# Clustered attention with an ELU network: the order of three kinds of VectorE work, and two blocks' row sums moved to VectorE

## The chip, the cores and the metric

The kernel runs on one core of a Trainium2 chip. The core has a matrix engine (TensorE, PE in the profile; its weight loads are listed as PEld), VectorE (DVE), ScalarE (ACT), GpSimd (POOL) and SyncE (SP, which only issues transfers here). Each engine works through its own list of instructions in order and waits on semaphores for the others. The metric is the device time of one execution in microseconds, lower is better.

## The reference

Inputs: q, k, v of shape (4 batches, 8 heads, 768 tokens, 64), 16 centroids a head, and two weight matrices 512 x 2048 and 2048 x 512. All are float64; the kernel turns them into float32.

```python
q_assign = np.argmax(np.einsum('bhsd,hcd->bhsc', q_n, c_n), axis=-1)   # q_n, k_n, c_n: normalised
k_assign = np.argmax(np.einsum('bhsd,hcd->bhsc', k_n, c_n), axis=-1)
mask = q_assign[:, :, :, None] == k_assign[:, :, None, :]
scores = np.where(mask, scale * q @ k^T, -1e9)
attn = exp(scores - max) / (sum + 1e-9)
x = (attn @ v), heads side by side                     # 3072 tokens x 512
h = x @ w_in
g = np.where(h > 0, h, np.exp(np.minimum(h, 0)) - 1)   # ELU
out = g @ w_out
```

A token of q attends only to the tokens of k that fall into the same cluster.

## The kernel before, in words

The work is cut into 48 blocks: 4 batches, 3 thirds of the queries (256 each), 4 pairs of heads. The loop at L795 runs over n, and each turn writes out by hand what every engine does next; no scheduler moves anything. In turn n:

- `values(n - 1)` multiplies the exponentials of the block before with v into `o_bank` (L581), and needs the sum of each row of exponentials. Either PE forms it with a matrix of ones (`row_sums`, L570: 12 small matmuls a block), or `sums(n)` has formed it on VectorE in three additions (L558, L559, L560, into the tile `psum`), and PE needs 2 matmuls. Then ScalarE (L599 to L602), VectorE (L603, L604) and POOL (L607) divide by the sum.
- `scores(n)` multiplies q and k in three units of 1024 columns (L499; in batch 0 also the mask, L511), each into one of three pairs of PSUM banks, and ScalarE takes the exponential (L522). In the later batches VectorE zeroes the other clusters afterwards (L457).
- `turn` transposes the q and k of the next batch on VectorE (L342).
- The network of the third that is LAG = 7 blocks back comes in groups of steps, four turns to a third. `hidden` (L617) multiplies x with a quarter of w_in into a pair of PSUM banks (L622), ScalarE takes the exponential (L632), POOL clips it (L633), and `elu` on VectorE joins the two (L639) and forms a difference (L641 or L643). The ELU is not issued at once: it is put on the list `lag`, and issued by the next `finish()`, which the next `hidden`, a step of its own, or the next turn calls. The ELU frees the PSUM banks of its slice. Two slices come in the turns with n - 7 divisible by 4, the other two and a `finish` in the turn after.
- `outer` (L660) then forms the product with w_out by seven products of halves instead of eight (L652), four in the third turn and three in the fourth. They use sums and differences of quarters of w_out (`sum_weights`, L322): t1, t2 and t4 in `w_sum`, and f_ overwritten by h_ - f_ in `w_out`. The third product needs the new f_, the fourth t4. The results pass through `o_bank` and `f_bank`, which ScalarE and VectorE empty (L686, L692, L697, L702); L687 and L693 update the ELU's halves.

The weights arrive as float64 words and are turned into float32 on VectorE and ScalarE in 34 steps (`weight_steps`, L265); `weigh(i)` issues i of them, three a turn in `scores` (L554) and some more in the turns 0, 7 and 8. In turn 8 `sum_weights` follows, in two halves, after all steps of the network.

Where `sums` stands in a turn: it is `late`, from turn 10 on, issued ahead of the network's steps or, in some turns, among them. At the end of a batch (turns 11, 23, 35; `extra[1]`, L857) VectorE is asked, after the second `hidden` of the turn, for the clusters of the next batch: `tell(b + 1, 0)` for q, the similarities of k (`clusters`: PE L377, VectorE L384), and `tell(b + 1, 1)` for k. A `tell` is six instructions on VectorE (twice L396, L400, L410) that leave `hot`. The next turn's `values` and `scores` follow, then `key_numbers` (L425), which reads k's `hot`, and `query_numbers` (L438).

Three pairs of banks go round. In the turn after a batch's end (12, 24, 36) the third unit of scores writes the pair that the second `hidden` of the turn before has used; in turn 9 the third unit writes the pair of the fourth `hidden` of turn 8 (L801, L803).

Of the kernel before, what the change touches and what calls it, by code (L numbers as in the profile page):

```python
# [15 lines left out]
Alu = mybir.AluOpType  # L16
# [45 lines left out]
def main_path(ctx, tc, c, q, k, v, centroids, moe_w_in, moe_w_out, out):  # L62
    nc = tc.nc
# [34 lines left out]
    def banks(i=None):  # L98
        nonlocal turn_of
        if i is None:  # L100
            i = turn_of
            turn_of = (turn_of + 1) % 3
        return pair_tiles[i % 3]
# [66 lines left out]
    for e in range(2):  # L170
# [5 lines left out]
            op=Alu.add,  # L176
# [27 lines left out]
    for e in range(2):  # L204
# [11 lines left out]
        op=Alu.mult,  # L216
# [90 lines left out]
    def weigh(n):  # L307
        for _ in range(n):
            next(rest, None)
# [7 lines left out]
    def w_parts():  # L317
        e_, f_ = w_out[:, : FC // 2, :QS], w_out[:, : FC // 2, QS:]
        g_, h_ = w_out[:, FC // 2 :, :QS], w_out[:, FC // 2 :, QS:]
        return e_, f_, g_, h_  # L320

    def sum_weights(half):  # L322

        of = slice(half * FC // 4, (half + 1) * FC // 4)
        e_, f_, g_, h_ = (x[:, of] for x in w_parts())
        t1, t2, t4 = (w_sum[:, n, of] for n in range(3))
        nc.vector.tensor_tensor(t1, f_, e_, op=Alu.subtract)
        nc.gpsimd.tensor_tensor(f_, h_, f_, op=Alu.subtract)
        nc.vector.tensor_tensor(t2, h_, t1, op=Alu.subtract)
        nc.vector.tensor_tensor(t4, g_, t2, op=Alu.subtract)  # L330

# [83 lines left out]
    def side(pr, e):  # L415
        return int(pr // 2 != e)
# [66 lines left out]
    LAG = 7  # L483
# [7 lines left out]
    def scores(n):  # L491
        b, third, pr = blocks[n]
        i = b * NPR + pr
        cols = ts(third, QS)

        def plain(s, kt):
            for e in range(2):
                rows = slice(64 * e, 64 * e + 64)
                nc.tensor.matmul(  # L499
                    s[:, e, ts(kt % 2, QS)],  # L500
                    lhsT=T[i, 1][rows, ts(kt, P)],
                    rhs=T[i, 0][rows, cols],
                    start=n > 0 or kt % 2 == 0,
                    stop=b > 0,
                    skip_group_check=n == 0,
                )

        def mask(s, kt):
            for e in range(2):
                rows = slice(64 * e, 64 * e + 64)  # L510
                nc.tensor.matmul(  # L511
                    s[:, e, ts(kt % 2, QS)],
                    lhsT=hot[b, 1][rows, side(pr, e), ts(kt, P)],
                    rhs=qm[n][rows],
                    start=False,
                    stop=True,
                    skip_group_check=n == 0,
                )

        def exponentials(s, u):  # L520
            p = pu[n, u] = probs.tile([P, 2, 2 * QS], F32, name="p", tag="p")
            nc.scalar.activation(p, s, Act.Exp, scale=SCALE)  # L522

        if n == 0:

            turn_first = similar(0, 1, 0, QS, o_bank)
            turn_rest = similar(0, 1, QS, 2 * QS, f_bank)
            units = [banks() for _ in range(2)]
            for u in range(2):
                for m in range(2):  # L530
                    plain(units[u], 2 * u + m)
            turn_first()
            for u in range(NT // 2):
                assign(0, 1, u * QS, QS)
                if u == 0:
                    turn_rest()
                if u == 1:
                    units.append(banks())
                    for m in range(2):
                        plain(units[2], 4 + m)  # L540
                for m in range(2):
                    mask(units[u], 2 * u + m)
                exponentials(units[u], u)
                weigh(1)
            return
        for u in range(NT // 2):
            s = banks(place["u"][u])
            for m in range(2):
                plain(s, 2 * u + m)
                if b == 0:  # L550
                    mask(s, 2 * u + m)
            exponentials(s, u)
            if n < LAG + 3:
                weigh(1)  # L554

    def sums(n):
        to = osum[n] = work.tile([P, 2, 2 * QS], F32, name="psum", tag="psum", bufs=1)
        nc.vector.tensor_tensor(to, pu[n, 0], pu[n, 1], op=Alu.add)  # L558
        nc.vector.tensor_tensor(to, to, pu[n, 2], op=Alu.add)  # L559
        nc.vector.tensor_tensor(to[:, :, :QS], to[:, :, :QS], to[:, :, QS:], op=Alu.add)  # L560
# [51 lines left out]
    def finish():  # L612
        for step in lag:
            step()
        lag.clear()
# [126 lines left out]
    def clusters(b, j, i):  # L742
        ps = banks(i)
        for turn_half in [similar(b, j, half * HS, HS, ps[:, half]) for half in range(2)]:
            turn_half()

    def tell(b, j):
        for half in range(2):
            assign(b, j, half * HS, HS)
# [45 lines left out]
    for n in range(len(blocks) + LAG):  # L795
        b, at = n // NB, n % NB
        ahead = b + 1 < B

        kind = (n - LAG) % 4 if n >= LAG else None
        if kind == 1:  # L800
            place.update(d=at_tile, u=[at_tile + 1, at_tile, at_tile + 2], h=[at_tile + 1, at_tile])  # L801
        elif kind == 2:
            place.update(d=at_tile + 2, u=[at_tile + 1, at_tile + 2, at_tile])  # L803
        else:
            place.update(d=at_tile, u=[at_tile + 1, at_tile + 2, at_tile])
            place.update(h=[at_tile + 1, at_tile + 2])
        if kind not in (0, 1):
            at_tile += 1
        if n > LAG:
            finish()  # L810
        if n <= len(blocks) and n > 0:
            values(n - 1)
        finish()
        if ahead:
            for pr in {5: [0], 6: [1], 9: [2], 10: [3]}.get(at, []):
                load("q", (b + 1) * NPR + pr)
                load("k", (b + 1) * NPR + pr)
        if n + 1 < len(blocks):
            load_v(n + 1)
        early = 0 < n < LAG + 3  # L820
        more = n + 1 < len(blocks) and at + 1 < NB
        if more and early:
            masks(n + 1)
        if n < len(blocks):
            scores(n)
        if more and not early:
            masks(n + 1)
        if n == 0:
            weigh(3)
        if n < len(blocks):  # L830
            if ahead and at in turns:
                for j in range(2):
                    turn((b + 1) * NPR + turns[at], j)
        main = groups[n - LAG] if n >= LAG else []
        extra = {}
        if n < len(blocks):
            late = [lambda n=n: sums(n)] if n >= LAG + 3 else []
            if b > 0:
                third = at // NPR
                q_in = lambda b, third, places: (lambda: query_numbers(b, third, places))  # L840
                if at == 0:
                    key_numbers(b)
                    query_numbers(b, third, [(0, o_bank)])
                    extra[0] = [q_in(b, third, [(1, f_bank), (2, o_bank)])]
                    extra[1] = [q_in(b, third, [(3, f_bank)])]
                elif at % NPR == 0:
                    query_numbers(b, third, [(0, f_bank), (1, o_bank)])
                    extra[0] = [q_in(b, third, [(2, f_bank), (3, o_bank)])]
                keep_same(n)
            if b > 0 and at % NPR == 2:  # L850
                extra[1] = late
            elif not ahead or at + 1 < NB:
                late and late[0]()
        if ahead and at + 1 == NB:

            extra[0] = [lambda b=b, i=place["u"][2]: clusters(b + 1, 0, i)] + late
            extra[1] = [  # L857
                lambda b=b: tell(b + 1, 0),
                lambda b=b, i=place["h"][0]: clusters(b + 1, 1, i),
                lambda b=b: tell(b + 1, 1),  # L860
            ]
        for m, step in enumerate(main):
            step()
            for other in extra.get(m, []):
                other()
            if n < LAG + 2 and m < 2:
                weigh(2 if n == LAG else 1)
        if n == LAG + 1:
            weigh(100)
            for half in range(2):  # L870
                sum_weights(half)
        if n == len(blocks) + 1:
            findings()
        if n == len(blocks) + 2:
            verdict()
# [254 lines left out]
```

## Time and profile before

| | |
|---|---|
| median of 8 runs | 1010.68 us |
| lowest, highest | 1009.28, 1013.11 us |
| the eight | 1011.15, 1010.20, 1010.98, 1012.61, 1009.91, 1010.38, 1009.28, 1013.11 |
| the profiled execution | 1013.1 us, its span 1010.9 us |
| mean granted clock of TensorE | 0.992 |
| PE busy | 990.1 us (98%) |
| VectorE busy | 657.3 us (65%) |
| ScalarE busy | 322.8 us (32%) |
| POOL busy | 135.5 us (13%) |
| L570 with p, 240 records | 37.2 us |
| L570 with psum, 152 records | 22.9 us |

A float32 matmul leaves two records, so that 12 row-sum matmuls are 24 records. All times in the trace are microseconds from the start of the span. In a timeline a row gives start, duration, engine, line, operation, output <- inputs, shapes and how often; a bracket gives how long the engine stood idle before it, and what ended that. Turns 8, 9 and 10 of the loop lie at about 108 to 132, 132 to 155 and 155 to 174 us. The three ends of a batch lie at about 188 to 208, 430 to 448 and 668 to 686 us.

### The profile page before, as it was taken

What the parts mean: (1) busy time and instruction counts of PE and PEld (TensorE: products, weight loads), DVE (VectorE), ACT (ScalarE), POOL (GpSimd) and SP (SyncE); (2) the same over time, 40 slices, a digit from 0 to 9 for tenths busy, and PEclk for the clock granted to TensorE, in tenths of its full rate; (3) what the DMA queues carried; (4) which work ended last, traced back from release to release, by engine and by line L of the source; (5) the groups of instructions that cost most, each with busy time, mean ns of one, the idle gap of its engine ahead of it and who ended that gap; (6) DMA issues with size and microseconds to landing.
All of it is one profiled execution on the core that took longest, in us unless ns stands there. A gap on an engine that the chain in (4) does not pass through costs nothing.

```text
span 1010.9 us, 14691 instructions
## 1 busy us (share of the span) xinstructions
PE 990.1 (98%) x5989; PEld 774.2 (77%) x5989; DVE 657.3 (65%) x1182; ACT 322.8 (32%) x576; POOL 135.5 (13%) x145
## 2 busy tenths in 40 slices
PE   6999999999999999999999999999999999999997
PEld 4566777767877877868788788777887887888886
DVE  7999973556756766787567467677666665673131
ACT  6777422223233232223232232124224223321010
POOL 0010130110210210111111111111021021021010
PEclk9899999989999999999999999999999999999999
DMA  9857122001123122100122113010011010100000
GB/s 290 315 162 191 56 53 63 18 16 32 37 47 64 37 48 48 52 17 17 53 43 52 39 39 70 30 27 29 16 38 31 17 37 17 32 21 1 22 1 24
DMA packets 103962, 55.58 MB, mean 55 GB/s; under 512 B 83408, under 2 KB 96720, under 8 KB 103888
## 3 DMA queue, kind: packets, MB, share of 16 engines
q1 hardware_dynamic: 103888, 54.57, 19.8%
q8 instruction: 49, 0.80, 0.3%
q14 instruction: 25, 0.20, 0.1%
HBM read 48.27 MB, written 6.29 MB: 54 GB/s over the span
## 4 chain that ended last, share of the span: by engine, by line
PE 81%; DVE 15%; issue 1%; ACT 1%; DMA 0%; POOL 0%; SPq 0%; DVEq 0%; POOLq 0%; ACTq 0%
PE banks L622 29%; PE f_bank L652 16%; PE o_bank L652 12%; PE banks L499 10%; PE o_bank L581 10%; PE banks L570 2%; DVE ex L272 2%; DVE gT L639 1%; DVE w_in L275 1%; DVE w_out L275 1%; DVE w_in L278 1%; DVE ex L294 1%; DVE w_out L278 1%; DVE oh L400 1%; DVE hot L410 1%
## 5 line engine op out<-in xcount | busy, mean ns | idle before, releaser
L622 PE MATMUL banks<-xT,w_in 128*128 128x256 f32 x1536 | 343.0, 383 | 0.3 <-POOL xT L607 0.3
L622 PEld LDWEIGHTS banks<-xT,w_in 128*128 128x128 f32 x1536 | 290.5, 191 | 49.0 <-issue 9.9
L457 DVE SCALAR_TENSOR_TENSOR p<-qc,kc,p 128x256 f32<-128x256 uint8 x432 | 183.9, 498 | 15.4 <-ACT qc L446 15.3
L499 PE MATMUL banks<-qT,kT 64*128 64x256 f32 x1152 | 147.5, 390 | 4.5 <-DVE gT L639 4.5
L581 PE MATMUL o_bank<-p,v_raw 128*64 128x256 f32 x1152 | 145.1, 386 | 1.5 <-ACT p L522 1.5
L639 DVE SCALAR_TENSOR_TENSOR gT<-gT,banks 128x1024 f32<-128x1024 f32 x48 | 58.4, 1216 | 131.7 <-POOL gT L633 131.7
L522 ACT ACTIVATE p<-banks 128x1024 f32<-128x1024 f32 x144 | 139.5, 1036 | 5.4 <-PE banks L499 4.7
L632 ACT ACTIVATE gT<-banks 128x1024 f32<-128x1024 f32 x48 | 49.1, 1023 | 285.2 <-PE banks L622 279.4
L499 PEld LDWEIGHTS banks<-qT,kT 64*128 64x128 f32 x1152 | 101.5, 187 | 43.0 <-issue 17.8
L581 PEld LDWEIGHTS o_bank<-p,v_raw 128*64 128x64 f32 x1152 | 78.2, 137 | 55.6 <-issue 14.5
L633 POOL TENSOR_SCALAR gT<-gT 128x1024 f32<-128x1024 f32 x48 | 52.7, 1098 | 336.8 <-ACT gT L632 331.0
L607 POOL TENSOR_TENSOR xT<-xT,r 128x256 f32<-128x256 f32 x48 | 40.7, 849 | 416.7 <-DVE r L604 367.5
L599 ACT ACTIVATE r<-banks 128x256 f32<-128x256 f32 x48 | 18.4, 383 | 243.3 <-PE banks L570 243.3
L652 PE MATMUL o_bank<-w_out,gT 128*128 128x256 f32 x416 | 95.1, 382 | 0.0
L652 PEld LDWEIGHTS o_bank<-w_out,gT 128*128 128x128 f32 x416 | 78.2, 190 | 13.5 <-issue 3.3
L652 PE MATMUL f_bank<-w_out,gT 128*128 128x256 f32 x352 | 79.6, 379 | 0.0
L603 DVE TENSOR_TENSOR e<-e,r 128x256 f32<-128x256 f32 x48 | 20.4, 424 | 86.5 <-ACT r L602 86.5
L652 PEld LDWEIGHTS f_bank<-w_out,gT 128*128 128x128 f32 x352 | 66.9, 190 | 9.1
L652 PE MATMUL f_bank<-w_sum,gT 128*128 128x256 f32 x224 | 50.9, 380 | 0.3 <-DVE o_sb L692 0.2
L559 DVE TENSOR_TENSOR psum<-psum,p 128x1024 f32<-128x1024 f32 x38 | 50.2, 1321 | 1.4
L652 PEld LDWEIGHTS f_bank<-w_sum,gT 128*128 128x128 f32 x224 | 42.3, 190 | 7.1 <-DVE o_sb L692 1.5
L558 DVE TENSOR_TENSOR psum<-p 128x1024 f32<-128x1024 f32 x38 | 46.0, 1212 | 0.0
(134 smaller groups left out, 838.0 us busy)
## 6 DMA issues: line engine op xcount, KB each, us to landing
v_raw<-in_v_dram SPq DMA_DIRECT2D x48, 384.0 KB, 3.2
w_sum<-in_moe_w_out_dram SPq DMA_DIRECT2D x12, 512.0 KB, 4.7
out_dram<-o_sb SPq DMA_DIRECT2D x24, 256.0 KB, 2.0
q_raw<-in_q_dram SPq DMA_DIRECT2D x48, 96.0 KB, 3.2
k_raw<-in_k_dram SPq DMA_DIRECT2D x48, 96.0 KB, 3.0
w_sum<-in_moe_w_in_dram SPq DMA_DIRECT2D x8, 512.0 KB, 8.6
w_out<-in_moe_w_in_dram SPq DMA_DIRECT2D x8, 512.0 KB, 10.8
w_out<-in_moe_w_out_dram SPq DMA_DIRECT2D x4, 512.0 KB, 3.8
```

The source lines that it names most:

```text
L457: nc.vector.scalar_tensor_tensor(p, qc[b, third][:, 2 * pr + e], kc[b][:, 2 * u + m, 2 * pr + e : 2 * pr + e + 1], p, op0=Alu.is_equal, op ...
L499: nc.tensor.matmul(s[:, e, ts(kt % 2, QS)], lhsT=T[i, 1][rows, ts(kt, P)], rhs=T[i, 0][rows, cols], start=n > 0 or kt % 2 == 0, stop=b > 0 ...
L522: nc.scalar.activation(p, s, Act.Exp, scale=SCALE)
L558: nc.vector.tensor_tensor(to, pu[n, 0], pu[n, 1], op=Alu.add)
L559: nc.vector.tensor_tensor(to, to, pu[n, 2], op=Alu.add)
L581: nc.tensor.matmul(o_bank[64 * e : 64 * e + 64, :QS], lhsT=raw["v", n][:, e, kt], rhs=p[:, e, ts(m, QS)], start=(kt == 0), stop=(kt == NT ...
L607: nc.gpsimd.tensor_tensor(x, x, r, op=Alu.mult)
L622: nc.tensor.matmul(hf[:, f], lhsT=w_in[:, ch, ts(4 * n + f, P)], rhs=xT[b, third][:, ch], start=(ch == 0 and f % 2 == 0), stop=(ch == KC - 1),
L632: nc.scalar.activation(t, hf, Act.Exp)
L633: nc.gpsimd.tensor_scalar(t, t, 1.0, 0.0, op0=Alu.min, op1=Alu.max)
L639: nc.vector.scalar_tensor_tensor(t, t, -1.0, hf, op0=Alu.add, op1=Alu.max)
L652: nc.tensor.matmul(to[:, :QS], lhsT=left[:, f], rhs=right[:, f], start=(f == 0), stop=(f == FC // 2 - 1),)
```

## The change

Four edits in one:

- In `sum_weights` the new f_ is formed by VectorE instead of POOL.
- `sum_weights` is issued inside turn 8, its first half after the second `hidden` of that turn (whose `finish` has issued the ELU of the slice before), its second half after the last ELU, instead of both after it.
- `sums` is asked for from turn 8 on instead of turn 10. So the rows of blocks 8 and 9 are summed by VectorE, in turns 8 and 9, after the transposes and ahead of the network's steps; PE has 2 matmuls instead of 12 for each.
- At the end of a batch `finish` is called ahead of the last `tell`, so that the ELU of the second slice is issued before k's clusters are told, and not after.

The limit of `weigh(1)` in `scores` goes from turn 9 to turn 8.

```diff
@@ sum_weights
         nc.vector.tensor_tensor(t1, f_, e_, op=Alu.subtract)
-        nc.gpsimd.tensor_tensor(f_, h_, f_, op=Alu.subtract)
+        nc.vector.tensor_tensor(f_, h_, f_, op=Alu.subtract)
         nc.vector.tensor_tensor(t2, h_, t1, op=Alu.subtract)
@@ scores
             exponentials(s, u)
-            if n < LAG + 3:
+            if n < LAG + 2:
                 weigh(1)
@@ the loop over n
         if n < len(blocks):
-            late = [lambda n=n: sums(n)] if n >= LAG + 3 else []
+            late = [lambda n=n: sums(n)] if n > LAG else []
...
             extra[1] = [
                 lambda b=b: tell(b + 1, 0),
                 lambda b=b, i=place["h"][0]: clusters(b + 1, 1, i),
+                finish,
                 lambda b=b: tell(b + 1, 1),
             ]
         for m, step in enumerate(main):
...
             if n < LAG + 2 and m < 2:
                 weigh(2 if n == LAG else 1)
-        if n == LAG + 1:
-            weigh(100)
-            for half in range(2):
-                sum_weights(half)
+            if n == LAG + 1 and m > 0:
+                weigh(100)
+                sum_weights(m - 1)
```

## The prediction

> **What bounds the kernel now.** I read the page's busy shares first, then the list of waits, then the timeline around each wait of TensorE (PE). The page:
>
> ```profile
> PE 990.1 (98%) x5989; PEld 774.2 (77%) x5989; DVE 657.3 (65%) x1182; ACT 322.8 (32%) x576; POOL 135.5 (13%) x145
> ```
>
> PE is the bound almost everywhere, so only PE instructions that vanish and PE's few waits are worth time. VectorE (DVE) and POOL work counts only where PE waits for it. The waits of PE on the lines touched:
>
> ```profile
> PE banks L499 <- DVE gT L639: 4.5, 4, 2.0
> PE f_bank L652 <- DVE o_sb L692: 0.2, 1, 0.2
> ```
>
> The first row: PE waits four times for the ELU (L639) to free a PSUM bank for scores. Three of these are the batch boundaries (timeline; columns are start, duration, work, and in brackets the idle time before it):
>
> ```profile
> 200.82 0.51 DVE L396 TENSOR_REDUCE top<-sim 128x24 f32<-128x384 f32 x1
> 204.12 1.18 DVE L639 SCALAR_TENSOR_TENSOR gT<-gT,banks 128x1024 f32<-128x1024 f32 x1
> 205.36 1.93 PE L499 MATMUL banks<-qT,kT 64*128 64x256 f32 x8 [1.97 <-DVE gT L639]
> 207.47 0.60 PE L438 MATMUL o_bank<-hot,index 32*128 32x256 bf16 x2
> 208.01 9.32 PE L622 MATMUL banks<-xT,w_in 128*128 128x256 f32 x32
> ...
> 446.26 1.13 PE L499 MATMUL banks<-qT,kT 64*128 64x256 f32 x8 [1.04 <-DVE gT L639]
> 447.57 0.39 PE L438 MATMUL o_bank<-hot,index 32*128 32x256 bf16 x2
> 447.89 7.17 PE L622 MATMUL banks<-xT,w_in 128*128 128x256 f32 x32
> ```
>
> The ELU, ready since POOL's clip ended at 198.94, stands behind the six assignment instructions that begin at 200.82. After the 1.97 us gap the same 32 matmuls take 9.32 us, after a 1.04 us gap 7.17. The table by stage says why: the granted clock fell (last but two columns).
>
> ```profile
> 203.00:206.00 3.00, 1.03 (x8) 0.57 (x6) 2.91 (x6) 1.60 (x2) 0.00 (x0) 0.93 0.21 77
> 206.00:208.00 2.00, 2.00 (x15) 0.85 (x12) 0.80 (x4) 0.68 (x1) 0.73 (x1) 0.50 0.00 0
> ```
>
> Last the stage of the weight sums:
>
> ```profile
> 126.08 1.04 POOL L633 TENSOR_SCALAR gT<-gT 128x1024 f32<-128x1024 f32 x1 [6.94 <-ACT gT L632]
> 132.98 1.04 POOL L633 TENSOR_SCALAR gT<-gT 128x1024 f32<-128x1024 f32 x1 [5.86 <-DMA k_raw<-in_k_dram]
> 134.05 1.22 DVE L639 SCALAR_TENSOR_TENSOR gT<-gT,banks 128x1024 f32<-128x1024 f32 x1 [4.95 <-POOL gT L633]
> 137.22 3.38 POOL L328 TENSOR_TENSOR w_out<-w_out 128x1024 f32<-128x1024 f32 x1 [3.20 <-DVE w_sum L327]
> 138.43 3.26 DVE L330 TENSOR_TENSOR w_sum<-w_out,w_sum 128x1024 f32<-128x1024 f32 x1
> 150.95 0.42 DVE L692 TENSOR_TENSOR o_sb<-f_bank,part 128x256 f32<-128x256 f32 x1
> 151.42 3.72 PE L652 MATMUL f_bank<-w_sum,gT 128*128 128x256 f32 x16 [0.24 <-DVE o_sb L692]
> ```
>
> DVE stands idle for 4.95 us ahead of the last ELU; L330, elsewhere like L329 1.23 us, takes 3.26 beside POOL's L328: the two exclude each other. DVE's list ends with L692 just in time for PE.
>
> **The change part by part.** The profiled execution took 1013.1 us (span 1010.9 and 2.2 around it), 2.4 above the median of 1010.68. I keep that difference apart, because the clock drop above may be the reason.
>
> 1. Row sums of blocks 8 and 9. With sums on PE a block takes from 155.07 (first L581) to 160.40 (first L499), 5.33 us; with a DVE sum 174.42 to 177.59, 3.17. PE loses 2.16 us a block, 4.32 in all. DVE gains two triples L558 to L560, 3.09 us each start to start (190.76 to 193.85).
>
> 2. L328 on DVE. I take 1.25 us as L327 to L329 (135.91 to 137.17) with the same strided operands; the other end is POOL's 3.38. Two instructions, 2.5 us more on DVE, but L330 falls from 3.26 to about 1.25, twice, 4.0 less. POOL's next work, L607 at 148.35, waits for DVE's L604 in any case, so POOL's freed time is worth nothing itself.
>
> 3. DVE's new list from 126.68, where the second L342 transpose ends, by starts: clip on POOL until 127.12, so the first sum starts 0.44 late; sum of block 8 3.09; ELU of slice 2 with its difference 1.86 (134.05 to 135.91); first weight half 5.0; in it the clip of slice 3 (ready at 132.98) takes its turn, 0.75 to 1.0, as L560 beside a clip took 1.44 for 0.69 at 456.35. The last ELU then starts at 138.0 and ends at 139.2, against 135.27 before.
> Behind it on DVE: the difference 0.6, second half 5.0, L603 and L604 0.8, two transposes 1.76, sum of block 9 3.09, L687 1.10, L692 0.42: L692 ends at 152.0, against 151.37.
>
> 4. Who waits. PE ends the third hidden slices at 131.77 as before, values of block 8 and two score units reach 131.77 + 3.17 + 2.17 = 137.1. The third unit writes the bank that the last ELU frees: PE waits to 139.3, 2.2 us (0.8 if neither clip holds up DVE). It then does 1.07 of scores and starts the first output product at 140.4, against 140.56: block 8's gain is gone. The fourth product needs L692: it starts at 152.05, 0.6 later than before, with a wait of 1.1 instead of 0.24. Block 9's 2.16 is kept, since its sum is ready by 150.5 and read after 158. Stage: 2.16 - 0.6 = 1.5 us gained. Ends: 3.0 (both clips harmless, DVE 1.4 earlier, L692 at 150.6, fourth product on time), and -2.8 if L328 costs its POOL price twice (4.3 more on DVE). The SP loads behind the transposes (149.09) are released 2 us earlier and used 10 us later: nothing.
>
> 5. Boundaries. The ELU and its difference (1.82, 204.12 to 205.94) move ahead of six instructions of the last assignment. At 446: PE runs on without the 1.04 gap, and reaches the key numbers (L425) at 446.2. Three of the six need the first half of the assignment (445.2, there), three the second, now 445.11 + 1.82 = 446.93. L438 starts at about 447.10 instead of 447.57: 0.47, likewise at 684. So the wait moves to L425, 0.6 us. At 204: assignment ends at 206.02, L438 at 206.2; before, at full clock, 205.36 + 1.07 + 0.24 = 206.67: 0.48, with a wait of about 1.5 us left. L603 and L457 follow the same total of DVE work, so nothing behind is later. The clock: 205.36 to the last L438 at 224.75 is 19.39, at 446.26 to 462.42 16.16, so the drop cost 3.23; it goes too if 1.5 us is too short to bring it.
>
> 6. The shorter list of conversion steps at block 9 issues nothing: all 34 steps are used up by the scores of block 8.
>
> Sum: 1.5 + 3 x 0.47 = 2.9 us, and 3.23 more in an execution that had the clock drop. From the profiled one: 1013.1 - 6.15 = 1006.95. From the median, if it stands for executions without the drop: 1010.68 - 2.9 = 1007.8. The 2.4 between them and the two of eight runs above 1012.6 speak for a drop in some executions only, so I take 1007.8.
>
> The clock decides most of the rest. In this trace a gap of 1.97 brought half clock, two of 0.95 close together near 25 us did so too, gaps of 1.04 did not. So my new 2.2 us gap can bring it.
> The Trainium skill (TensorE: Matmul & The Clock Gate, HAM oscillation) speaks of PE gaps of over about 3.4 us; by that neither the old nor the new gap should bring a drop, the 3.23 would not have been lost, and the sum would be 2.9 in every execution. The trace shows half clock after 1.97, so the row decides.
>
> **The rivals.**
>
> - Clock drop at the new gap. Price 3.23, of which 1.1 fills the wait for L692: 2.1 lost. 1007.8 + 2.1 = 1009.9 (1006.7 if the old drop was in the median). For it: 2.2 exceeds 1.97. Against: eight runs lie mostly low although the 1.97 gap must be in them.
> - The old drop is in the median run, and goes: 1010.68 - 6.15 = 1004.5.
> - Slower: DVE becomes the bound of the stage. If L328 keeps 3.38 us on DVE, L692 ends at 156.3 and the stage loses 2.8; with a clock drop that the 4.4 us gap brings at its start mostly covered by the same wait, 1 us more: 1010.68 + 3.8 - 1.4 = 1013.1. It decides from L692 at 151.4 + 2.16 + 1.4 = 155.0 on. Against it: L327 and L329 read the same rows at 1.2.
> - The wait only moves: at the boundaries L425 waits as long as L499 did and the stage nets nothing: 1010.5.
>
> **How the numbers follow.** Chances: forecast 0.40, old drop gone 0.18, new drop 0.22, DVE bound 0.13, wait only moved 0.07. About 0.2%, 2 us, is what can be told from no change. Faster: most of the forecast, old drop gone and a third of new drop, 0.61; slower: most of DVE bound and tails, 0.14; the same 0.25. The range 1004.2 to 1012.0 leaves out half of DVE bound and tails; the forecast's own is 1006.3 to 1009.2.
>
> **What would show it.** Right: block 8 and 9 with 24 L581 and then 4 L570 in one piece; L330 near 1.23; DVE without the 4.95 idle; a PE gap of about 2 us at L499 near 137 named after L639; L692 near 152; no L499 wait at the boundaries, but one of 0.6 to 1.5 at L425; L622 after the first boundary 7.2 instead of 9.3. Wrong: L328 above 2 us, half clock near 140, or half clock still at 206.

## The result, and the profile after

The changed kernel takes 1007.81 us (median of 12 runs, 1006.17 to 1008.81), the kernel before 1011.40 us (median of 34 runs beside it, 1008.95 to 1013.71). The ratio, taken over all runs and not from the two medians, is 0.9963, with a 95% interval of 0.9954 to 0.9972: 0.37% faster. The lower edge of the runs fell by 2.8 us and the upper by 4.9 us, so the runs also lie closer together. The profiled execution took 1007.47 us, its span 1005.4.

From the page after, the busy shares (engine, busy us, share, instructions):

```profile
PE 982.8 (98%) x5949; PEld 770.8 (77%) x5949; DVE 661.9 (66%) x1190; ACT 323.5 (32%) x576; POOL 130.2 (13%) x143
```

PE lost 40 records, VectorE gained eight instructions, POOL lost two. This and the later views show only the rows that bear on the argument. From the list of waits after (who waited for what: total us, times, longest):

```profile
PE f_bank L425 <- DVE hot L410: 3.2, 4, 1.4
PE banks L499 <- DVE gT L639: 1.9, 2, 1.4
PE f_bank L652 <- DVE o_sb L692: 1.0, 2, 0.8
```

The three waits of L499 at the batch ends are gone; what is left of that row is an early wait of 0.5 us that stood there before, and a new one of 1.4. L425, which waited for no VectorE work before, now waits 3.2 us (1.42, 0.78 and 0.78 us at the three ends, and 0.22 us ahead of the first of these). The timeline of turns 8 and 9 after:

```profile
133.20 1.94 DVE L328 TENSOR_TENSOR w_out<-w_out 128x1024 f32<-128x1024 f32 x1
136.32 1.23 DVE L330 TENSOR_TENSOR w_sum<-w_out,w_sum 128x1024 f32<-128x1024 f32 x1
137.46 1.22 DVE L639 SCALAR_TENSOR_TENSOR gT<-gT,banks 128x1024 f32<-128x1024 f32 x1
138.73 0.70 PE L499 MATMUL banks<-qT,kT 64*128 64x256 f32 x4 [1.42 <-DVE gT L639]
150.96 0.42 DVE L692 TENSOR_TENSOR o_sb<-f_bank,part 128x256 f32<-128x256 f32 x1
151.43 3.72 PE L652 MATMUL f_bank<-w_sum,gT 128*128 128x256 f32 x16 [0.79 <-DVE o_sb L692]
158.26 0.70 PE L499 MATMUL banks<-qT,kT 64*128 64x256 f32 x4
```

PE waits 1.42 us for the last ELU and 0.79 us for L692, and starts the fourth product at 151.43, as before the change (151.42). The scores of turn 10 start at 158.26 instead of 160.40: one block's 2.14 us is kept (0.08 us of it PE was ahead before block 8), the other's was waited away. And the first batch end after:

```profile
198.68 1.18 DVE L639 SCALAR_TENSOR_TENSOR gT<-gT,banks 128x1024 f32<-128x1024 f32 x1
199.14 2.96 PE L499 MATMUL banks<-qT,kT 64*128 64x256 f32 x24
203.97 0.23 PE L425 MATMUL f_bank<-index,hot 128*128 128x8 bf16 x3 [1.42 <-DVE hot L410]
204.13 0.39 PE L438 MATMUL o_bank<-hot,index 32*128 32x256 bf16 x2
204.45 7.17 PE L622 MATMUL banks<-xT,w_in 128*128 128x256 f32 x32
```

The 24 records of scores run in one piece, the wait sits at L425, and the 32 hidden matmuls take 7.17 us: this execution kept full clock, where the profiled one of before took 9.32 us for them.

L438 at the three batch ends comes at 204.13, 441.70 and 679.07, against 207.47, 447.57 and 685.30: 3.34, 5.87 and 6.23 us earlier. PE's last products start 6.23 us earlier too (995.78 against 1002.01). The 6.23 us are 2.14 from the stage, 0.38, 0.37 and 0.37 from the ends, 3.2 that the clock drop of the profiled execution of before cost, less 0.2 lost between the first and the second end. The span is only 5.5 us shorter, since from the start of the last VectorE instruction (L723) to the end it took 6.0 us instead of 5.2; nothing in the change touches that, and it was not followed up.

### The profile page after: what moved, and what is told of

Same layout as the page of the kernel before. It is cut to its first block, busy times and chain, and to the rows that moved or that the text cites. A ratio compares the mean times of both kernels' runs of the same rounds, so it can differ in the third digit from the quotient of the medians.

```text
span 1005.4 us, 14617 instructions
## 1 busy us (share of the span) xinstructions
PE 982.8 (98%) x5949; PEld 770.8 (77%) x5949; DVE 661.9 (66%) x1190; ACT 323.5 (32%) x576; POOL 130.2 (13%) x143
## 4 chain that ended last, share of the span: by engine, by line
PE 79%; DVE 18%; ACT 1%; issue 1%; DMA 0%; DVEq 0%; ACTq 0%
PE banks L622 29%; PE f_bank L652 15%; PE o_bank L652 12%; PE o_bank L581 10%; PE banks L499 10%; DVE ex L272 2%; PE banks L570 2%; DVE w_out L275 1%; DVE gT L639 1%; DVE w_in L275 1%; DVE w_in L278 1%; DVE w_out L278 1%; DVE ex L294 1%; DVE oh L400 1%; DVE psum L559 1%
## 5 line engine op out<-in xcount | busy, mean ns | idle before, releaser
L499 PE MATMUL banks<-qT,kT 64*128 64x256 f32 x1152 | 146.1, 388 | 1.9 <-DVE gT L639 1.9
L499 PEld LDWEIGHTS banks<-qT,kT 64*128 64x128 f32 x1152 | 101.4, 186 | 39.4 <-issue 17.8
L559 DVE TENSOR_TENSOR psum<-psum,p 128x1024 f32<-128x1024 f32 x40 | 52.7, 1317 | 1.6
L558 DVE TENSOR_TENSOR psum<-p 128x1024 f32<-128x1024 f32 x40 | 48.8, 1220 | 0.0
```

The source lines that it names most:

```text
L499: nc.tensor.matmul(s[:, e, ts(kt % 2, QS)], lhsT=T[i, 1][rows, ts(kt, P)], rhs=T[i, 0][rows, cols], start=n > 0 or kt % 2 == 0, stop=b > 0 ...
```

## The experiments

All times are medians; each group of kernels had the kernel before run beside it on the same chip, and the ratio is to those runs. The median of before differs from group to group (1009.35 to 1011.40), its lowest run hardly (1008.84 to 1009.00), so kernels of different groups are compared here by their ratios and lowest runs as well as by their medians.

| kernel | time us | runs from, to | before us | ratio, 95% interval |
|---|---|---|---|---|
| changed kernel | 1007.81 | 1006.17, 1008.81 | 1011.40 | 0.9963, 0.9954 to 0.9972 |
| boundary edit alone | 1008.72 | 1007.88, 1009.90 | 1011.02 | 0.9980, 0.9969 to 0.9992 |
| all but the boundary edit | 1009.68 | 1007.22, 1010.70 | 1011.02 | 0.9983, 0.9970 to 0.9995 |
| row sums alone | 1014.13 | 1012.75, 1014.52 | 1011.02 | 1.0029, 1.0018 to 1.0041 |
| weights' sums alone | 1010.78 | 1008.38, 1012.66 | 1011.02 | 0.9998, 0.9985 to 1.0011 |
| changed, block 9 alone | 1007.09 | 1005.47, 1008.10 | 1009.35 | 0.9966, 0.9954 to 0.9979 |
| before, longer gaps | 1020.76 | 1017.46, 1022.40 | 1009.35 | 1.0101, 1.0082 to 1.0120 |
| changed, f_ on POOL | 1008.58 | 1007.73, 1010.05 | 1010.82 | 0.9981, 0.9972 to 0.9991 |
| changed, weights' sums behind | 1010.88 | 1008.87, 1012.02 | 1010.82 | 0.9999, 0.9990 to 1.0008 |
| changed, q's clusters early | 1004.01 | 1003.77, 1004.30 | 1009.35 | 0.9939, 0.9925 to 0.9953 |
| changed, all early | 1000.91 | 1000.77, 1001.21 | 1009.35 | 0.9908, 0.9893 to 0.9924 |

The theory under test had two parts. One: in turns 8 and 9 VectorE's list, up to L692, sets when PE goes on, so PE's vanished row sums count only as far as that list allows. Two: at a batch's end a PE gap of about 2 us costs its own length and, in some executions, several us at half clock. The rivals: PE's instruction count decides by itself; and the spread of the runs has nothing to do with the clock.

### The boundary edit alone

```diff
                 lambda b=b, i=place["h"][0]: clusters(b + 1, 1, i),
+                finish,
                 lambda b=b: tell(b + 1, 1),
```

> The boundary edit alone. My theory: L499's waits of 1.97, 1.04 and 1.04 us at the batch ends go, L425 waits 1.4, 0.8 and 0.8 us instead, and no clock drop follows the first end any more. Gain 1.2 us (0.48 and twice 0.37) in executions that had no drop, 4.5 us in those that had, so a median some 1.2 to 3 us below the median of before, and the runs no longer spread over 4 us: none above about 1011. Rival, the spread of the runs of before has nothing to do with the clock: 1.2 us in all, and some runs still near 1012.

Measured: 2.3 us faster, and no run above 1009.90 where before reached 1013.25. The lower edge moved by 1.0 us (1008.88 to 1007.88), the upper by 3.4. So a part of the gain is there in every execution and a larger one only in some, as the theory has it. The runs of before beside it say the same of the clock: 13 of the 34 took 1008.88 to 1009.45 us at a mean granted clock of 0.998, nine 1010.38 to 1011.50 at 0.995 to 0.998, and twelve 1012.25 to 1013.25 at 0.992 to 0.995. The rival, a spread that has nothing to do with the clock, does not fit that. But the theory's sentence that no drop follows the first end any more was too strong. Timeline, then the table by stage (granted clock in the last column but two), of this kernel's profile:

```profile
205.67 0.23 PE L425 MATMUL f_bank<-index,hot 128*128 128x8 bf16 x3 [1.42 <-DVE hot L410]
206.15 8.86 PE L622 MATMUL banks<-xT,w_in 128*128 128x256 f32 x32
```

```profile
206.00:208.00 2.00, 2.00 (x8) 1.52 (x7) 1.51 (x5) 0.72 (x2) 0.72 (x1) 0.69 0.00 0
208.00:210.00 2.00, 2.00 (x6) 1.53 (x5) 2.00 (x6) 0.00 (x0) 0.00 (x0) 0.50 0.00 0
210.00:212.00 2.00, 2.00 (x10) 1.78 (x9) 2.00 (x6) 0.00 (x0) 0.00 (x0) 0.95 0.00 0
```

Here the clock fell after the gap of 1.42 us at L425, which follows one of 0.21 us with only three small matmuls between. The clock is half for about 3.4 us (granted 0.69 in the first row, 0.50 in the second, 0.95 in the third), and that cost 8.86 - 7.17 = 1.7 us, not 3.2. The shorter gap does not exclude the drop. Five profiles of the study have it at the first end: two dropped, each for 3.4 us (this one and the weights' sums behind the last ELU), three did not.

### All edits but that one

The changed kernel without the line above.

> All edits but the one at the batch ends. My theory: block 9's 2.1 us are kept and block 8's are given back in a wait of 1.4 us for the last ELU and 0.8 us for L692, so 2.1 us faster; the gap of 1.97 us at the first batch end stays, and with it the clock drop of 3.2 us in some executions: the spread of about 4 us stays. Rival, the full 4.3 us of PE's vanished row sums: 1007.

Measured: 1.3 us between the medians, 1.7 us between the lower edges, ratio 0.9983; the runs spread over 3.5 us. That is less than the 2.1 us expected, though its profile shows these: the stage takes 26.56 us (131.32 to 157.88) against 28.63 before, with waits of 1.41 us at L499 and 0.79 for L692. What the runs lose of it was not traced. The batch end is the most telling pair of lines of the study:

```profile
202.83 1.13 PE L499 MATMUL banks<-qT,kT 64*128 64x256 f32 x8 [1.97 <-DVE gT L639]
204.45 7.17 PE L622 MATMUL banks<-xT,w_in 128*128 128x256 f32 x32
```

The same gap of 1.97 us as in the profile of before, at full clock behind it. Four profiles have this gap in this place. Two kept full clock (this one and the row sums alone), the one of before fell to half for 6.84 us, and the one with the weights' sums alone for 3.4 us:

```profile
204.53 1.13 PE L499 MATMUL banks<-qT,kT 64*128 64x256 f32 x8 [1.97 <-DVE gT L639]
206.15 8.86 PE L622 MATMUL banks<-xT,w_in 128*128 128x256 f32 x32
```

So one gap cost nothing, 1.7 us or 3.2 us behind it, which are about the distances between the three groups of runs above. Another stretch at half clock, near 25 us, stands in every profile of the study (3.4 or 6.84 us long); with either length the values of block 8 start between 131.1 and 131.8 us, so it can make no more than 0.7 us of the spread. This profile also gives the batch end's price without the clock: from the first score record to L438 5.37 us here (198.76 to 204.13) against 4.99 after the change (199.14 to 204.13), 0.38 us.

### The row sums alone

```diff
-            late = [lambda n=n: sums(n)] if n >= LAG + 3 else []
+            late = [lambda n=n: sums(n)] if n > LAG else []
```

> Only the row sums of blocks 8 and 9 move to VectorE; f_ stays on POOL and the weights' sums behind the last ELU. My theory: VectorE's list sets the time. L692 ends at about 154.5 instead of 151.4, the fourth product starts 3.1 us late after a gap of some 5 us, block 9 gives 2.1 back: 0.9 us slower, and up to 3.2 more where the gap brings the clock drop. Rival, PE's instructions set the time: 4.3 us faster.

Measured: 3.1 us slower, with 40 records fewer on PE. The fourth product:

```profile
153.97 6.38 PE L652 MATMUL f_bank<-w_sum,gT 128*128 128x256 f32 x16 [5.60 <-DVE o_sb L692]
```

It starts 2.5 us later than before, after a gap of 5.6 us, and takes 6.38 us where 3.72 is its time at full clock: 2.7 us more, at a granted clock of 0.50 from 154 to 158 us. Both prices of the theory are in this line, and the rival's 4.3 us gain is refuted.

### The weights' sums alone

The changed kernel with `sums` from turn 10 on as before, and without the boundary edit.

> Only the weights' sums change (f_ on VectorE, first half ahead of the last ELU); row sums of blocks 8 and 9 and the batch ends as before. My theory: PE waited 0.24 us here and waits no more, so 0.2 us faster, not to be told from no change. Rival, POOL and VectorE no longer exclude each other for 4 us and this is the gain: 2 to 4 us faster.

Measured: no difference (0.9998). Some 4 us in which POOL and VectorE shut each other out are gone, and the time does not move, since PE had waited only 0.24 us for that work. In the profile the stage is 0.5 us shorter (131.45 to 159.58, 28.13 against 28.63), less than the interval can show. Taken with the experiment before it, the edit is worth next to nothing alone and is what makes the row sums pay.

### Block 9's rows alone

```diff
-            late = [lambda n=n: sums(n)] if n > LAG else []
+            late = [lambda n=n: sums(n)] if n > LAG + 1 else []
```

> The changed kernel, but only block 9's rows are summed by VectorE; block 8's 10 matmuls are back on PE. My theory: block 8's 2.16 us only bought two waits of 1.42 and 0.79 us, so PE does the work in place of waiting and the time is that of the changed kernel within 0.3 us, with no wait at L499 near 138 and none for L692. Rival, each block's vanished matmuls count by themselves: 2.1 us slower than the changed kernel.

Measured: 0.9966, the changed kernel's 0.9963 within both intervals. In its profile L499 has no wait near 138, and the fourth product starts without a gap:

```profile
150.51 3.62 PE L652 MATMUL f_bank<-w_sum,gT 128*128 128x256 f32 x16
```

The stage, from the first values of block 8 to the scores of turn 10, takes 25.97 us (131.26 to 157.23), in the changed kernel 26.57 (131.69 to 158.26), before 28.63 (131.77 to 160.40). So moving block 8's sum to VectorE bought nothing: PE waits as long as it would have worked.

### Longer gaps

```diff
-        nc.vector.tensor_reduce(top, s, axis=Axis.X, op=Alu.max)
+        for _ in range(2 if b > 0 and j == 1 else 1):
+            nc.vector.tensor_reduce(top, s, axis=Axis.X, op=Alu.max)
```

> The kernel before, with each row maximum of the last assignment of a batch (L396, 0.51 us) taken twice, 1.06 us more ahead of the ELU: the gaps become 3.0, 2.1 and 2.1 us. My theory, a PE gap of about 2 us or more can bring half clock for some 6.8 us: 3.2 us for the gaps themselves and 3.2 us more for each drop, one at the first end almost always and one at the second and third in about half the executions: 5 to 9 us slower than before. Rival, the spread of the runs of before comes from elsewhere and gaps under 3.4 us keep the clock: 3.2 us slower, with full clock behind all three gaps.

Measured: 11.4 us slower, beyond the theory's 5 to 9. Lines of this kernel have numbers one higher. The second and third batch ends, which had kept full clock with 1.04 us:

```profile
448.29 1.75 PE L500 MATMUL banks<-qT,kT 64*128 64x256 f32 x8 [2.22 <-DVE gT L640]
450.76 9.49 PE L623 MATMUL banks<-xT,w_in 128*128 128x256 f32 x32
...
690.37 1.50 PE L500 MATMUL banks<-qT,kT 64*128 64x256 f32 x8 [2.21 <-DVE gT L640]
692.59 9.75 PE L623 MATMUL banks<-xT,w_in 128*128 128x256 f32 x32
```

Gaps of 2.2 us brought half clock at both (9.49 and 9.75 instead of 7.17 us), for some 6.8 us each. The first end, with a gap of 3.14 us, fell to half clock for as long. I had put the later two at half the executions; all six runs are 8.5 to 13.4 us above the lower edge of before, where the gaps themselves make 3.2. Three drops of 3.2 us and these 3.2 make 12.8, and the profiled execution, the slowest of the six, is 13.1 us above the median of before. The rival, which keeps the clock, is refuted.

### f_ back on POOL

```diff
-        nc.vector.tensor_tensor(f_, h_, f_, op=Alu.subtract)
+        nc.gpsimd.tensor_tensor(f_, h_, f_, op=Alu.subtract)
```

> The changed kernel with f_ = h_ - f_ back on POOL, all else as changed. My theory: POOL and VectorE exclude each other again, L330 takes about 3.26 us instead of 1.23, VectorE's list up to L692 grows by 0.8 us a half less the 0.7 us that L328 lost to the clip, so L692 and the fourth product come about 0.8 us later: 0.8 us slower than the changed kernel. Rival, VectorE's list gets two instructions (2.5 us) shorter and L692 comes earlier: up to 0.8 us faster.

Measured: 1008.58 against 1007.81, ratios 0.9981 and 0.9963, so 0.8 us slower by the medians and 1.8 by the ratios. In the profile:

```profile
133.66 3.33 POOL L328 TENSOR_TENSOR w_out<-w_out 128x1024 f32<-128x1024 f32 x1
134.80 3.27 DVE L330 TENSOR_TENSOR w_sum<-w_out,w_sum 128x1024 f32<-128x1024 f32 x1
139.26 0.70 PE L499 MATMUL banks<-qT,kT 64*128 64x256 f32 x4 [2.32 <-DVE gT L639]
140.59 5.32 PE L652 MATMUL o_bank<-w_out,gT 128*128 128x256 f32 x16
152.39 0.42 DVE L692 TENSOR_TENSOR o_sb<-f_bank,part 128x256 f32<-128x256 f32 x1
152.86 3.72 PE L652 MATMUL f_bank<-w_sum,gT 128*128 128x256 f32 x16
```

L330 is back at 3.27 us, and L692 comes 1.43 us later (1.8 later counted from the first values of block 8, at 131.32 here and 131.69 in the changed kernel). The expected 0.8 us had counted on 0.7 us that L328 would no longer lose beside the clip; in this kernel L329 stands there and takes 1.94 us in its place. The gap for the last ELU has grown to 2.32 us and the first product takes 5.32 instead of 3.72 us: a clock drop (granted clock 0.61 and 0.54 from 140 to 144), which is hidden because the fourth product could not start before L692 in any case. The other way round, in the changed kernel two VectorE instructions more made VectorE's list shorter.

### The weights' sums behind the last ELU

```diff
-            if n == LAG + 1 and m > 0:
-                weigh(100)
-                sum_weights(m - 1)
+        if n == LAG + 1:
+            weigh(100)
+            sum_weights(0), sum_weights(1)
```

> The changed kernel with both halves of the weights' sums behind the last ELU, f_ on VectorE. My theory: the last ELU ends at about 135.3 and the wait of 1.42 us at L499 goes, but VectorE stands idle for some 2 us before it and L692 ends 1.3 us later or less: the fourth product waits some 3 to 4 us and starts 0.9 us later, so 0.9 us slower than the changed kernel, and up to 3 us more where the longer gap brings the clock drop. Rival, the wait for the last ELU was the cost: 1.4 us faster.

Measured: 3.1 us slower than the changed kernel (3.6 by the ratios), no gain on before. The wait for the last ELU is gone, and the one for L692 grew:

```profile
133.82 1.22 DVE L639 SCALAR_TENSOR_TENSOR gT<-gT,banks 128x1024 f32<-128x1024 f32 x1 [1.94 <-POOL gT L633]
152.60 6.23 PE L652 MATMUL f_bank<-w_sum,gT 128*128 128x256 f32 x16 [3.80 <-DVE o_sb L692]
```

VectorE's 1.94 us of idling in front of the ELU come out at L692, 1.16 us late (152.12 to 150.96, the rest being the clip's collision that falls away), and the gap of 3.8 us brings half clock: 6.23 instead of 3.72 us, 2.5 more. 1.2 + 2.5 = 3.7 us is what this execution lost at the fourth product.

### q's clusters early

At a batch's end VectorE idles ahead of the transposes of q's similarities (L384), for 7.8 us at the first end and 2.5 us at the other two, and then is late for L425. (In this diff and the next the helper functions `clusters` and `sum_weights` get a parameter, which is not shown.)

```diff
-            extra[0] = [lambda b=b, i=place["u"][2]: clusters(b + 1, 0, i)] + late
-            extra[1] = [
-                lambda b=b: tell(b + 1, 0),
-                lambda b=b, i=place["h"][0]: clusters(b + 1, 1, i),
-                finish,
-                lambda b=b: tell(b + 1, 1),
-            ]
+            clusters(b + 1, 0, None, (f_bank, o_bank))
+            tell(b + 1, 0)
+            extra[0] = [lambda b=b, i=place["u"][2]: clusters(b + 1, 1, i)] + late
+            extra[1] = [lambda b=b: tell(b + 1, 1), finish]
```

> The changed kernel, but at a batch's end q's clusters go ahead of the first hidden slice (into f_bank and o_bank) and are told at once, k's go behind the first slice and are told ahead of the last ELU. My theory, what is left at the batch ends is VectorE's list being late for L425 by 1.64, 0.8 and 0.8 us, while it stood idle for 7.8 and 2.5 us ahead of q's transposes: with that work moved into the idle time L425 waits no more, 2.6 to 3.2 us faster than the changed kernel, and no clock drop behind the batch ends. Rival, the wait moves once more, to L499 for the last ELU or to L377 for the transposed q: less than 1 us.

Measured: 1004.01, which is 3.8 us below the changed kernel by the medians and 2.4 us both by the ratios and by the lowest runs (the two ran in different groups), and all runs within 0.53 us. Timeline at the first batch end:

```profile
199.19 2.97 PE L499 MATMUL banks<-qT,kT 64*128 64x256 f32 x24
199.22 1.18 DVE L639 SCALAR_TENSOR_TENSOR gT<-gT,banks 128x1024 f32<-128x1024 f32 x1
202.09 0.30 PE L425 MATMUL f_bank<-index,hot 128*128 128x8 bf16 x6
202.64 7.17 PE L622 MATMUL banks<-xT,w_in 128*128 128x256 f32 x32
```

Neither L499 nor L425 waits here, and the clock stays. The waits taken away are some 3.2 us; that the spread of 2.6 us shrank with them is what a drop behind L425 in some executions of the changed kernel would give. No profile of the changed kernel itself caught that drop; its runs go from 1006.17 us at a mean granted clock of 0.997 to 1008.81 at 0.994.

### All early

The same, with two more moves in turns 8 and 9: the last ELU goes ahead of all but two of the eight instructions of the weights' sums, and the sum of block 9's rows goes behind L693.

```diff
-            if n == LAG + 1 and m > 0:
-                weigh(100)
-                sum_weights(m - 1)
+            if n == LAG + 1 and m == 1:
+                weigh(100)
+                sum_weights(0, range(2))
+            if n == LAG + 1 and m == 2:
+                sum_weights(0, range(2, 4))
+                sum_weights(1)
...
-            if b > 0 and at % NPR == 2:
+            if b > 0 and at % NPR == 2 or n == LAG + 2:
                 extra[1] = late
```

> The kernel with q's clusters early, and in turns 8 and 9 the last ELU ahead of all but two of the weights' sums, and the sum of block 9's rows behind L693. My theory: the last ELU ends before PE reaches its bank near 137, L692 ends before the fourth product, and both waits (1.42 and 0.79 us) go: 2.0 us faster than with q's clusters early alone, about 1002. Rival, VectorE's list in turn 8 is full and a wait of 1 us or more stays for f_, t4 or L692: under 1 us faster.

Measured: 1000.91 (1000.77 to 1001.21), 3.1 us below the last one and 0.92% faster than the kernel before: the best of all.

```profile
134.83 1.21 DVE L639 SCALAR_TENSOR_TENSOR gT<-gT,banks 128x1024 f32<-128x1024 f32 x1
147.53 0.41 DVE L692 TENSOR_TENSOR o_sb<-f_bank,part 128x256 f32<-128x256 f32 x1
148.56 3.62 PE L652 MATMUL f_bank<-w_sum,gT 128*128 128x256 f32 x16
```

The last ELU ends at 136.0, L692 at 147.9, and PE waits for neither; the stage takes 23.82 us (131.46 to 155.28), against 26.57 in the changed kernel: both blocks' 2.16 us are kept, and the short wait for L692 that stood there before is gone as well. No VectorE instruction was added or taken away for it. It is 2.75 us of the 3.1; the remaining 0.35 was not traced. Expected were 2.0 us, from the two waits of 1.42 and 0.79; the stage gave 0.5 more than these.

## Why the prediction was right, and where it was not

**The number.** 1007.8 was forecast and 1007.81 measured, but the two parts behind it moved against each other. The median of before was 1010.68 in the eight runs shown and 1011.40 in 34, and the gain was 3.6 us instead of 2.9. The lower edges, where the clock dropped least, stand 2.8 us apart, close to the forecast sum of 2.9; the parts measured in the profiles are 2.1 for the stage and 1.1 for the ends, where 1.5 and 1.4 had been put down. The rest is the rival "the old drop goes", which I had as a separate case: it holds in a share of the executions, so the median takes some of it. That the two shifts cancel to 0.01 us is luck; the mechanism did not need it.

**Steps 1 to 4, the stage.** Right: block 9's row sums kept, block 8's waited away (shown by the run with block 9 alone), a new wait at L499 and one for L692. Too large was step 3's first weight half with the clip: 5.0 and 0.75 to 1.0 us put down, 5.51 measured from L327 to the last ELU (131.95 to 137.46), so the ELU started at 137.46 and not 138.0, and the gap was 1.42 instead of 2.2 us. That mattered: the clock stayed behind 1.42 us in the changed kernel's profile and fell behind the 2.32 us of the kernel with f_ on POOL, the price that the rival "clock drop at the new gap" had. L692 ended at 151.38 instead of 152.0, the fourth product was on time, and the stage gained 2.14 instead of 1.5 us.

**Step 2.** L328 has VectorE's time, as taken: 1.23 us in the second half, and 1.94 in the first, where POOL's clip held it up. POOL's 3.38 was not its price, and the slower rival that rested on it fell. Its mechanism, VectorE as the bound of the stage, is real: the run with the row sums alone and the one with the sums behind each lost to it.

**Step 5, the batch ends.** The wait moved to L425 with 1.42, 0.78 and 0.78 us (forecast 1.5, 0.6, 0.6). Without the clock each end gained 0.37 to 0.38 instead of 0.47 to 0.48. What did not hold is the hope that 1.5 us is too short to bring the drop: 1.42 us brought a short one in the boundary edit's profile. The 3.23 us put on the old drop took a start from the timeline and one from another view; by the timeline alone it is 19.33 - 16.16 = 3.17 us (205.36 to 224.69).

**Step 6** holds: there is no conversion instruction left in turn 9 in either kernel. (These steps concern the weights alone: of the inputs only the two weight matrices are float64, while q, k, v and the centroids are float32.)

**The clock.** The row decided rightly against the rule of the Trainium skill (TensorE: Matmul & The Clock Gate, HAM oscillation) that warns of gaps above about 3.4 us: here gaps of 1.42, 1.97, 2.2, 2.3 and 3.8 us all brought half clock in some execution. Another statement of that page (The HAM clock gate) fits better: the activity window is about 3.4 us long and free-running, and the moment at which the clock is released depends on where in it the first matmul falls. The page says this of the release only; that a fall of the clock is a matter of the window as well is argued here, not shown. For it speak that every half-clock stretch ahead of the last products in the twelve profiles lasts 3.4 us (as in the boundary edit) or 6.8 us (as in before and with the longer gaps), and that one gap of 1.97 us had and had not a drop; no run shows the window itself.

In the profiles PE's lead over before shrinks by 0.21 us between 225 and 437 us, outside the changed places: PE waits 0.22 us for L692 at 391.26, where it does not wait before. Why VectorE is late there stays open.

## What to carry to other kernels

When one engine is the bound, price the work taken off it against the list of the engine that receives it, up to the first instruction the bound engine waits for: here two equal savings were worth 2.1 us and nothing, and a mere reordering later brought the second back. Look for idle time of the receiving engine ahead of the late instruction, and move the work that could already run into it, not just past its neighbour. Price a wait of the matrix engine with what its clock does afterwards, and judge it by the edges of many runs, since one profile shows only one outcome.

## What was not expected of the hardware

A PE gap of 2.2 us cost more than itself: with 1.06 us more at three places the kernel lost 11.4 us, about 3.2 of them in the gaps. And one and the same gap of 1.97 us was followed by full clock in two executions, by 3.4 us at half clock (1.7 us lost) in a third and by 6.84 us (3.2 us lost) in a fourth, so that the run-to-run spread of 4 to 5 us of the kernel before is mostly that of a few short waits: with the waits at the batch ends gone, runs lie within 0.5 us of each other.
